# An LSH attention and two MoE layers on one core: both readers of a bucket-count bank on one engine, the scaled q written in one GpSimd pass, and a new written order

## The chip, the core and the metric

One core of one Trainium2 chip runs the whole program. The metric is device time in microseconds (us): the median of a few executions, each from launch to end. The engines are named as the profile names them: PE (TensorE, matmuls), PEld (its weight loads), DVE (VectorE), ACT (ScalarE), POOL (GpSimd) and SP (SyncE, which issues the DMAs). Each engine works through its own queue in order; they wait for one another through semaphores.

## The reference, cut to what matters

```python
# q, k, v: (2 batches, 8 heads, 768 positions, 64); proj: (64, 6)
q_bits = (q @ proj > 0);  k_bits = (k @ proj > 0)          # 6 bits = 64 buckets
mask   = q_bucket[:, :, :, None] == k_bucket[:, :, None, :]
scores = where(mask, q @ k.T / 8, -1e9)
attn   = exp(scores - max);  attn /= attn.sum() + 1e-9
x  = (attn @ v), heads joined: 1536 tokens x 512
x  = silu_moe(rmsnorm(x))      # 512 -> 1536 -> 512: gate, val, out
out = elu_moe(x)               # 512 -> 2048 -> 512: in, out
```

All of it is float32. The kernel gets that precision from fast matmuls by splitting an operand into a high part (rounded to the PE's fp32r type) and a low part (what the rounding lost).

## The kernel before, in words

The 16 heads are taken as 8 pairs (`j`); a pair has two heads (`a` = 0, 1). For each pair SP loads three layouts of q and k, and `prep` makes from them the operands of the score matmul. `prep_bits` (L434) projects q and k on PE (`ps_b`), and DVE turns the result into bits (`bitt`). `prep_count` (L455) multiplies the bits with a table on PE: each bank `ps_c` holds, for 384 positions, the number of agreeing bits with each of the 64 buckets, rows 0 to 63 for head 0 and rows 64 to 127 for head 1. Two instructions read such a bank, one for each head, and write the "hot" part of the operand: `tq` for i = 0 (q), `tk` for i = 1 (k). The engine of each of the two is `HOT[2 * i + a]` (L28, L479): before, head 0 of q and head 1 of k on DVE (L472), the others on ACT (L470). The program makes two readers of one bank on different engines wait for each other, in the written order.

`operand_k` (L369) writes the high part of k on ACT (L375) and the low part on POOL (L382). `operand_q` (L393) writes the high part of q. All 128 rows hold the same 64 dimensions twice; the upper 64 rows are to be q and the lower 64 rows q / 8. Before, POOL did this in two instructions, a plain cast of the upper half (L405) and a multiplication of the lower half (L412). SP then copies the lower half to its second place (`dup`, L416), and POOL replaces the upper half by the low part (L420).

`score` (L504) runs four matmuls `ps_s` for each 128 queries: the first two use the first plane of the operands (high and low parts), the other two the second plane (hot and `dup`). DVE takes the maximum (L524), ACT the exponential (L534). There are two double banks for `ps_s`, so the third score waits until the first exponential has read its bank. `turn` (L550) transposes the weights on PE (`ps_p`) and splits them on ACT (L570) and DVE (L574), for some units through POOL (L579 to L586). `weigh` (L597) multiplies with v (`ps_v`). After the attention come the norm and the two MoE layers (`ps_h`, `ps_y`, `ps_o`), which are nearly all matmuls.

What sets the order: every piece of work is a task, added to a plan with its engine and the keys that it reads and writes. `run` (L218) emits the tasks in the order of a written list of numbers, `ORDER` (L33); the costs in `plan.add` were used to find that list and do nothing at run time. The order on each engine's queue follows from it. A DMA that waits holds all later DMAs of SP's queue.

Of the kernel before, what the change touches and what calls it, by code (L numbers as in the profile page):

```python
# [27 lines left out]
HOT = ('DVE', 'ACT', 'ACT', 'DVE')  # L28
BW = (384, 512)
QENG = ["Pool"] * 16  # L30
# [195 lines left out]
def kernel(  # L226
# [76 lines left out]
    def dve(n):  # L303
        return n / 960.0 + 0.069
# [64 lines left out]
    def operand_k(j, a, cols, prio):  # L369
# [10 lines left out]
        def lo():  # L380
# [9 lines left out]
            [okey(j, a, 1, ("lo", h)) for h in cols], prio,  # L390
        )

    def operand_q(j, a, cols, prio, how):  # L393
        cs = slice(cols[0] * HS, (cols[-1] + 1) * HS)
        X_ = ("h3", "x", j, a, 2)
        n = HS * len(cols)
# [877 lines left out]
```

## Time and profile before

| | |
|---|---|
| median of 3 executions | 839.86 us (838.7 to 840.76) |
| profiled execution, its own time | 840.58 us |
| its span, first to last instruction | 838.8 us |
| PE busy | 816.9 us (97%) |
| DVE busy | 602.1 us (72%) |
| ACT busy | 416.8 us (50%) |
| POOL busy | 328.1 us (39%) |
| granted TensorE clock, mean over the span | 0.996 |

The shares are means over stages that differ. The first 280 us are the attention, in which PE, DVE, ACT and POOL are all busy most of the time; from there to the end PE is busy nearly without a break and the others have room. The end of a matmul is modelled, so that a short pause between two matmuls does not show as idle time. A granted clock of 1.00 stands for 2.4 GHz and 0.50 for 1.2 GHz.

### The profile page before, as it was taken

To read this page: it belongs to the slowest core of one execution; us is meant where nothing else is said; L and a number is where in the kernel's file an instruction comes from. 1 tells how busy PE (TensorE), PEld (TensorE's weight loads), DVE (VectorE), ACT (ScalarE), POOL (GpSimd) and SP (SyncE) were. 2 spreads that over 40 slices of the span, in tenths; PEclk is the share of its full clock that TensorE was granted. 3 is DMA by queue.
4 is the path that set the end of the run, shared out by engine and by line. 5 is a ranking of instruction groups with operands and counts; after the bars stand their busy time and mean duration, and the time that the engine had idled before them with its cause. 6 is when DMAs were issued, how large, how long until landed. Compare 5 with 4: busy or idle time off the path is not lost.

```text
span 838.8 us, 11843 instructions
## 1 busy us (share of the span) xinstructions
PE 816.9 (97%) x4498; PEld 714.1 (85%) x4498; DVE 602.1 (72%) x933; ACT 416.8 (50%) x785; POOL 328.1 (39%) x273
## 2 busy tenths in 40 slices
PE   7999999999899999999999999999999999999998
PEld 6898888888789999898888888888788888888887
DVE  4788899999998683543555564879666768677676
ACT  3898998977888553431222321335454242332321
POOL 7899987898988501100111212021012011110210
PEclk8999999999999999999999999999999999999999
DMA  6525842252103002200302123130322300021004
GB/s 214 165 68 169 275 143 83 67 159 69 39 1 114 1 1 93 71 26 1 131 21 76 51 61 115 39 103 13 111 76 87 102 24 26 26 76 50 1 1 150
DMA packets 28473, 64.99 MB, mean 77 GB/s; under 512 B 2816, under 2 KB 3584, under 8 KB 28416
## 3 DMA queue, kind: packets, MB, share of 16 engines
q1 hardware_dynamic: 28416, 64.24, 23.8%
q8 instruction: 35, 0.57, 0.3%
q14 instruction: 22, 0.18, 0.1%
HBM read 57.94 MB, written 3.15 MB: 73 GB/s over the span
## 4 chain that ended last, share of the span: by engine, by line
PE 77%; DVE 11%; ACT 7%; issue 2%; POOL 1%; DMA 1%; SPq 0%; ACTq 0%; DVEq 0%; POOLq 0%
PE ps_h L949 36%; PE ps_o L1089 15%; PE ps_y L1034 10%; PE ps_v L609 5%; PE ps_s L517 5%; PE ps_p L562 4%; DVE pt L574 2%; DVE nm L524 2%; ACT p L534 2%; ACT pt L570 2%; PE ps_b L442 1%; DVE wf L867 1%; DMA kk<-in_heads_dram 1%; DVE wf L874 1%; DVE ya L1046 1%
## 5 line engine op out<-in xcount | busy, mean ns | idle before, releaser
L900 POOL TENSOR_TENSOR wlo<-wf,whi 128x768 fp32r<-128x768 f32 (+1 forms) x54 | 88.4, 1650 | 448.3 <-ACT whi L896 387.4
L949 PE MATMUL ps_h<-xn,whi 128*128 128x512 f32 (+2 forms) x768 | 190.2, 336 | 0.0
L949 PEld LDWEIGHTS ps_h<-xn,whi 128*128 128x128 f32 x768 | 133.8, 189 | 11.9
L995 ACT CAST h<-hf 128x512 fp32r<-128x512 f32 (+1 forms) x87 | 52.1, 606 | 179.3 <-DVE hf L980 60.5
L949 PE MATMUL ps_h<-xn,wlo 128*128 128x512 f32 (+2 forms) x384 | 128.9, 336 | 0.0
L1089 PE MATMUL ps_o<-whi,h 128*128 128x512 f32 (+1 forms) x388 | 118.6, 387 | 0.4 <-DVE ya L1046 0.4
L949 PE MATMUL ps_h<-y,whi 128*128 128x512 f32 x384 | 118.2, 389 | 0.0
L517 PE MATMUL ps_s<-tk,tq 128*128 128x384 f32 x384 | 90.8, 359 | 8.7 <-ACT p L534 6.4
L609 PE MATMUL ps_v<-pt,vv 128*128 128x256 f32 x576 | 94.4, 294 | 2.1 <-DVE pt L574 1.0
L524 DVE TENSOR_REDUCE nm<-ps_s 128x1 f32<-128x768 f32 x96 | 90.8, 947 | 7.4 <-PE ps_s L517 6.5
L999 DVE TENSOR_TENSOR h<-hf,h 128x512 fp32r<-128x512 f32 (+1 forms) x87 | 64.5, 756 | 41.5 <-ACT h L995 41.3
L1034 PE MATMUL ps_y<-h,whi 128*128 128x512 f32 (+1 forms) x312 | 91.6, 374 | 0.8 <-DVE ya L1046 0.7
L534 ACT ACTIVATE p<-ps_s,nm 128x768 f32<-128x768 f32 x96 | 87.1, 908 | 8.5 <-DVE nm L524 7.7
L574 DVE TENSOR_TENSOR pt<-ps_p,pt 128x512 fp32r<-128x512 f32 x120 | 80.0, 682 | 12.9 <-ACT pt L570 12.0
L562 PE MATMUL ps_p<-ident,p 128*128 128x128 f32 x576 | 84.6, 278 | 2.9 <-DVE pt L574 2.2
L1089 PEld LDWEIGHTS ps_o<-whi,h 128*128 128x128 f32 x388 | 72.6, 188 | 15.5 <-DVE ya L1046 0.8
L974 ACT ACTIVATE sg<-ps_h 128x512 f32<-128x512 f32 (+1 forms) x87 | 49.4, 580 | 72.3 <-PE ps_h L949 53.3
L949 PEld LDWEIGHTS ps_h<-y,whi 128*128 128x128 f32 x384 | 72.1, 188 | 14.9
L609 PEld LDWEIGHTS ps_v<-pt,vv 128*128 128x128 f32 x576 | 78.8, 189 | 5.4 <-DVE pt L574 2.2
L562 PEld LDWEIGHTS ps_p<-ident,p 128*128 128x128 f32 x576 | 67.6, 142 | 12.0 <-DVE pt L574 5.1
L949 PEld LDWEIGHTS ps_h<-xn,wlo 128*128 128x128 f32 x384 | 72.6, 189 | 5.7
L517 PEld LDWEIGHTS ps_s<-tk,tq 128*128 128x128 f32 x384 | 64.3, 191 | 14.9 <-ACT p L534 10.8
(91 smaller groups left out, 1366.4 us busy)
## 6 DMA issues: line engine op xcount, KB each, us to landing
wraw<-in_moe_w_out_dram SPq DMA_DIRECT2D x12, 768.0 KB, 4.7
qq<-in_heads_dram SPq DMA_DIRECT2D x16, 384.0 KB, 4.2
qk<-in_heads_dram SPq DMA_DIRECT2D x16, 384.0 KB, 4.7
kk<-in_heads_dram SPq DMA_DIRECT2D x16, 384.0 KB, 4.0
wraw<-in_moe_w_in_dram SPq DMA_DIRECT2D x8, 768.0 KB, 5.6
wraw<-in_moe_w_out_dram SPq DMA_DIRECT2D x10, 512.0 KB, 3.6
vn<-in_v_dram SPq DMA_DIRECT2D x8, 384.0 KB, 3.5
wraw<-in_moe_w_gate_dram SPq DMA_DIRECT2D x4, 768.0 KB, 5.4
```

Of the source, the lines that this page charges most:

```text
L517: nc.tensor.matmul(st[B_][:, hf, 0:HS], lhsT=tq[:, x, c * 128:(c + 1) * 128], rhs=tk[:, x, hf * HS:(hf + 1) * HS], start=(x == 0), stop=(x ...
L524: nc.vector.tensor_reduce(out=st["nm", u, cc], in_=st[B_][:, :, 0:HS], axis=AX.XY, op=ALU.max, negate=True,)
L534: nc.scalar.activation(out=halves(st["p", u][:, cc]), in_=st.pop(B_)[:, :, 0:HS], func=AF.Exp, bias=st["nm", u, cc], scale=1.0, accum_out= ...
L562: nc.tensor.transpose(out=st[B_][:, o:o + 128], in_=p[:, cc, (2 * n + kt) * 128:(2 * n + kt + 1) * 128], identity=ident,)
L574: nc.vector.tensor_tensor(out=pt[:, 1], in0=st.pop(B_), in1=f(pt[:, 0]), op=ALU.subtract)
L609: nc.tensor.matmul(st[B_][:, 0:256], lhsT=st["vv", j][:, a, 2 * n + kt, :], rhs=pt[:, x, kt * 256:(kt + 1) * 256], start=(n == seq[0] and ...
L900: nc.gpsimd.tensor_tensor(out=l, in0=s["w"], in1=f(h), op=ALU.subtract)
L949: nc.tensor.matmul(ps[:, o:o + ln], lhsT=w[wp][:, kk, ft * 128:(ft + 1) * 128], rhs=t[xp][:, s:s + ln], start=(kk == 0 and n == 0), stop=( ...
L995: nc.scalar.copy(out=st["h", g, blk, ft][:, 0, 0:bw], in_=s["hf"])
L999: nc.vector.tensor_tensor(out=h[:, 1, 0:bw], in0=s["hf"], in1=f(h[:, 0, 0:bw]), op=ALU.subtract)
L1034: nc.tensor.matmul(s["ps"][:, 0:bw], lhsT=wo[wp][:, ft, m * 128:(m + 1) * 128], rhs=h[:, xp, 0:bw], start=(ft == 0 and i == 0), stop=(ft = ...
L1089: nc.tensor.matmul(s["ps"], lhsT=h[:, xp, t * 128:(t + 1) * 128], rhs=wo[wp][:, ft, ds], start=(ft == 0 and i == 0), stop=(ft == n - 1 and ...
```

## The change

Three things are edited. `HOT` gets one engine for each bank: DVE reads both heads of q, ACT both heads of k. `operand_q` writes the high part of q by one POOL instruction over 128 rows, with a factor for each row (`share`, 1 in the upper half and 1/8 in the lower) and a second factor of 1.0. `ORDER` is a new list; a few costs that were used to find it are changed too, and do nothing at run time. No matmul is added or taken away.

```diff
-HOT = ('DVE', 'ACT', 'ACT', 'DVE')
+HOT = ('DVE', 'ACT')
-QENG = ["Pool"] * 16
 ORDER = [
-    9, 0, 6, 5, 1, 7, 56, 50, 53, 2, 8, 48, 51, 57, 59, 49, 28, 10, 12, 13, 14, 15, 16, 17, 54, 55, 11, 60, 61, 68,
...
-    def operand_q(j, a, cols, prio, how):
+    def operand_q(j, a, cols, prio):
...
         def both():
-            nc.scalar.activation(
-                out=operand(j, a, 0)[:, 0, cs], in_=st["x", j, a, 2][:, cs], func=AF.Copy, scale=share[:, 1:2]
-            )
-
-        def upper():
-            out, in_ = operand(j, a, 0)[up, 0, cs], st["x", j, a, 2][up, cs]
-            nc.gpsimd.tensor_copy(out=out, in_=in_)
-
-        def lower():
-            out, in_ = operand(j, a, 0)[dn, 0, cs], st["x", j, a, 2][dn, cs]
-            if how == "mixed":
-                nc.scalar.activation(out=out, in_=in_, func=AF.Copy, scale=QSCALE)
-            else:
-                nc.gpsimd.tensor_scalar(out=out, in0=in_, scalar1=QSCALE, scalar2=None, op0=ALU.mult)
+            nc.gpsimd.tensor_scalar(
+                out=operand(j, a, 0)[:, 0, cs], in0=st["x", j, a, 2][:, cs], scalar1=share[:, 1:2], scalar2=1.0,
+                op0=ALU.mult, op1=ALU.mult,
+            )
...
-        if how == "ACT":
...
-            plan.add("Pool", 0.12 + n * 0.00092, upper, [X_], los, prio)
...
-                plan.add("Pool", 0.12 + n * 0.00092, lower, [X_], his, prio)
+        plan.add("Pool", 0.17 + n * 0.00105, both, [X_, "share"], his + los, prio)
...
         for a in range(2):
-            eng = HOT[2 * i + a]
+            eng = HOT[i]
```

Three places show what moves. The first is ACT at the start of the program, before the change; `tk` and `tq` are operands (110 and 101 of head 0, 131 and 134 of head 1), `kk` is loaded k, `ps_c` a count bank, `p` the weights.

```order
L375 ACTIVATE tk_110<-kk_108,share_86 128x384 [waits DMAHW4_49,DVE_49]
L375 ACTIVATE tk_110<-kk_108,share_86 128x384
L375 ACTIVATE tk_131<-kk_118,share_86 128x384 [waits DMAHW6_49]
L470 ACTIVATE tk_110<-ps_c_163 64x384 [waits PE_49]
L470 ACTIVATE tk_110<-ps_c_168 64x384 [waits PE_49]
L470 ACTIVATE tq_134<-ps_c_171 64x384 [waits PE_49]
L470 ACTIVATE tq_134<-ps_c_160 64x384
L534 ACTIVATE p_199,sums_200<-ps_s_183,nm_190 128x768 [waits DVE_49]
L534 ACTIVATE p_199,sums_200<-ps_s_192,nm_197 128x768 [waits DVE_49]
L375 ACTIVATE tk_131<-kk_118,share_86 128x384
```

ACT at the same place after the change (`tk_134` is of head 0, `tk_162` of head 1).

```order
L373 ACTIVATE tk_134<-kk_132,share_86 128x384 [waits DMAHW4_49,DVE_49]
L373 ACTIVATE tk_134<-kk_132,share_86 128x384
L451 ACTIVATE tk_134<-ps_c_142 64x384 [waits PE_49]
L451 ACTIVATE tk_134<-ps_c_152 64x384 [waits PE_49]
L451 ACTIVATE tk_162<-ps_c_152 64x384
L373 ACTIVATE tk_162<-kk_149,share_86 128x384 [waits DMAHW7_49]
L515 ACTIVATE p_184,sums_185<-ps_s_167,nm_172 128x768 [waits DVE_49]
L515 ACTIVATE p_184,sums_185<-ps_s_176,nm_182 128x768 [waits DVE_49]
L373 ACTIVATE tk_162<-kk_149,share_86 128x384
L451 ACTIVATE tk_162<-ps_c_142 64x384
```

The two `tq` readers are gone from ACT, and the cast of head 1's k (`kk_118`, now `kk_149`), which stood ahead of all readers of the counts, now stands behind three of them and ahead of the first exponential.

The second place is SP at the start, before the change: the loads, and the copies `tq<-tq` (`dup`).

```order
L322 DMA qq_89<-in_heads_dram 128x768
L322 DMA qk_92<-in_heads_dram 128x768
L1144 DMA pj_80<-in_proj_dram 128x256
L322 DMA qk_99<-in_heads_dram 128x768
L322 DMA kk_108<-in_heads_dram 128x768
L1137 DMA wtmp_116<-in_table_dram 128x256
L322 DMA kk_118<-in_heads_dram 128x768
L322 DMA qq_129<-in_heads_dram 128x768
L416 DMA tq_101<-tq_101 64x384 [waits DMAHW0_49,Pool_49]
L416 DMA tq_101<-tq_101 64x384 [waits DMAHW1_49,Pool_49]
L333 DMA vn_174<-in_v_dram 128x768 [waits DMAHW2_49]
L322 DMA qk_188<-in_heads_dram 128x768 [waits DMAHW3_49]
```

SP at the start after the change.

```order
L320 DMA qk_89<-in_heads_dram 128x768
L320 DMA qk_94<-in_heads_dram 128x768
L1125 DMA pj_80<-in_proj_dram 128x256
L320 DMA qq_127<-in_heads_dram 128x768
L320 DMA kk_132<-in_heads_dram 128x768
L1118 DMA wtmp_139<-in_table_dram 128x256
L404 DMA tq_129<-tq_129 64x384 [waits Pool_49]
L320 DMA kk_149<-in_heads_dram 128x768
L320 DMA qq_157<-in_heads_dram 128x768 [waits DMAHW0_49]
L331 DMA vn_165<-in_v_dram 128x768 [waits DMAHW1_49]
L404 DMA tq_129<-tq_129 64x384 [waits DMAHW2_49,Pool_49]
L320 DMA qk_236<-in_heads_dram 128x768 [waits DMAHW3_49]
```

Both `qk` now go first, `qq` of head 0 falls from the first place to the fourth, and the first `dup` stands ahead of the second `kk`, the second `qq` and `vn`, which wait in the queue until it has been issued.

The third place is PE at the counts of the last pair (some 214 us into the trace of before), before the change.

```order
L609 MATMUL ps_v_2823<-pt_2758,vv_1941 128x256 x4
L609 MATMUL ps_v_2823<-pt_2813,vv_1941 128x256 [waits Activation_49]
L609 MATMUL ps_v_2823<-pt_2813,vv_1941 128x256
L609 MATMUL ps_v_2823<-pt_2813,vv_1941 128x256 [waits DVE_49]
L609 MATMUL ps_v_2823<-pt_2813,vv_1941 128x256
L461 MATMUL ps_c_2842<-bitt1_83,wsel_81 128x384 [waits PE_49]
L461 MATMUL ps_c_2845<-bitt1_83,wsel_81 128x384 [waits DVE_49]
L461 MATMUL ps_c_2853<-bitt1_83,wsel_81 128x384 [waits Activation_49]
L517 MATMUL ps_s_2857<-tk_2465,tq_2342 128x384 [waits Activation_49]
L517 MATMUL ps_s_2857<-tk_2465,tq_2342 128x384 x3
```

PE at the counts of the last pair, after the change.

```order
L498 MATMUL ps_s_2796<-tk_2360,tq_2309 128x384 x4
L442 MATMUL ps_c_2803<-bitt1_83,wsel_81 128x384 [waits DVE_49]
L590 MATMUL ps_v_2808<-pt_2770,vv_1875 128x256 [waits DVE_49]
L590 MATMUL ps_v_2808<-pt_2770,vv_1875 128x256 x3
L590 MATMUL ps_v_2808<-pt_2745,vv_1875 128x256 x4
L442 MATMUL ps_c_2817<-bitt1_83,wsel_81 128x384 [waits DVE_49]
L442 MATMUL ps_c_2819<-bitt1_83,wsel_81 128x384 [waits PE_49,Activation_49]
L590 MATMUL ps_v_2808<-pt_2784,vv_1875 128x256 x4
L543 MATMUL ps_p_2827<-ident_79,p_2662 128x128 [waits DVE_49]
L543 MATMUL ps_p_2827<-ident_79,p_2662 128x128 x3
L442 MATMUL ps_c_2836<-bitt1_83,wsel_81 128x384 [waits DVE_49,PE_49]
L498 MATMUL ps_s_2849<-tk_2360,tq_2309 128x384 [waits Activation_49]
```

Three of the four `ps_c` stood in a row, with no other work between them and the next score; now at most two stand together, with `ps_v` and `ps_p` between, and a score ahead of all four.

## Rows read from the trace of the kernel before

**Rows 1.** Stretches: us, busy us (instructions) of each engine, PEclk, DMA share, GB/s.
```profile
14.90:21.70 6.80, 5.69 (x22) 5.09 (x21) 4.64 (x6) 3.45 (x7) 6.27 (x8) 0.50 0.27 76
20.00:120.00 100.00, 96.62 (x657) 87.33 (x656) 85.34 (x131) 87.96 (x179) 94.62 (x80) 0.99 0.54 171
120.00:260.00 140.00, 131.32 (x900) 117.25 (x900) 132.45 (x200) 118.12 (x242) 119.48 (x103) 1.00 0.21 63
280.00:820.00 540.00, 538.86 (x2667) 464.76 (x2667) 349.35 (x545) 185.10 (x319) 81.58 (x52) 1.00 0.17 54
```

**Rows 2.** Waits of PE: who waited for whom, us in total, times, longest.
```profile
PE ps_s L517 <- ACT p L534: 6.4, 9, 1.4
...
PE ps_s L517 <- DVE tq L472: 2.1, 1, 2.1
```

**Rows 3.** Waits of the bank readers for each other, in the same columns.
```profile
ACT tq L470 <- DVE tq L472: 5.9, 6, 1.3
...
DVE tq L472 <- ACT tq L470: 4.1, 4, 2.5
ACT tk L470 <- DVE tk L472: 3.7, 4, 1.5
...
DVE tk L472 <- ACT tk L470: 2.8, 3, 1.7
```

**Rows 4.** Timeline of the start: start us, us, engine, line, what, [idle before, releaser].
```profile
2.09 0.43 SPq L322 DMA_DIRECT2D qk<-in_heads_dram  x1
...
8.16 2.20 PE L442 MATMUL ps_b<-qk,pj 128*128 128x384 f32 x6 [0.77 <-DMA qk<-in_heads_dram]
...
9.18 1.12 ACT L375 ACTIVATE tk<-kk,share 128x384 fp32r<-128x384 f32 x2 [7.19 <-DMA kk<-in_heads_dram]
...
11.13 0.61 ACT L375 ACTIVATE tk<-kk,share 128x384 fp32r<-128x384 f32 x1 [0.83 <-DMA kk<-in_heads_dram]
...
12.52 0.87 ACT L470 ACTIVATE tq<-ps_c 64x384 fp32r<-64x384 f32 x2
...
13.42 0.55 DVE L472 TENSOR_SCALAR tq<-ps_c 64x384 fp32r<-64x384 f32 x1 [2.47 <-ACT tq L470]
...
14.07 1.55 PE L517 MATMUL ps_s<-tk,tq 128*128 128x384 f32 x6 [2.10 <-DVE tq L472]
...
16.73 2.93 PE L517 MATMUL ps_s<-tk,tq 128*128 128x384 f32 x8 [1.11 <-ACT p L534]
```

**Rows 5.** Groups by line and shape: count, busy us, mean ns, idle before.
```profile
L412 POOL TENSOR_SCALAR tq<-qq 64x768 fp32r<-64x768 f32 x14 | 29.9, 2133 | 1.2
...
L405 POOL CAST tq<-qq 64x768 fp32r<-64x768 f32 x14 | 11.9, 848 | 0.4
...
L412 POOL TENSOR_SCALAR tq<-qq 64x384 fp32r<-64x384 f32 x4 | 4.7, 1170 | 0.3
...
L382 POOL TENSOR_TENSOR tk<-kk,tk 64x384 fp32r<-64x384 f32 x4 | 3.9, 999 | 0.2
...
L741 POOL TENSOR_SCALAR z<-z 128x384 f32<-128x384 f32 x2 | 1.0, 514 | 0.2
```

**Rows 6.** The copies `tq<-tq` of L416, by line.
```profile
DMA to landing us min/median/max: 2.0/2.8/5.9
```

**Rows 7.** The loads of L322, by line.
```profile
DMA to landing us min/median/max: 2.8/4.4/8.6
```

**Rows 8.** Timeline at the counts of the last pair.
```profile
215.32 1.17 DVE L472 TENSOR_SCALAR tq<-ps_c 64x384 fp32r<-64x384 f32 x2
215.45 0.62 PE L461 MATMUL ps_c<-bitt,wsel 128*128 128x384 f32 x2 [1.04 <-DVE pt L574]
215.89 0.49 ACT L470 ACTIVATE tq<-ps_c 64x384 fp32r<-64x384 f32 x1 [1.14 <-DVE tq L472]
216.39 0.90 ACT L534 ACTIVATE p<-ps_s,nm 128x768 f32<-128x768 f32 x1
...
217.43 0.97 PE L517 MATMUL ps_s<-tk,tq 128*128 128x384 f32 x4 [1.36 <-ACT p L534]
```

More of the change, by code (lines that the diff above doesn't have):

```diff
@@ L422, in operand_q @@
         his, los, dups = ([okey(j, a, 0, (p, h)) for h in cols] for p in ("hi", "lo", "dup"))
-        if how == "ACT":
-            plan.add("ACT", act(n) + 0.15, both, [X_, "share"], his + los, prio)
-        else:
-            plan.add("Pool", 0.12 + n * 0.00092, upper, [X_], los, prio)
-            if how == "mixed":
-                plan.add("ACT", act(n) + 0.05, lower, [X_], his, prio)
-            else:
-                plan.add("Pool", 0.12 + n * 0.00092, lower, [X_], his, prio)
+        plan.add("Pool", 0.17 + n * 0.00105, both, [X_, "share"], his + los, prio)
         dma(dup, 64 * n * 4, his, dups, prio)
@@ L478, in prep_count @@
         for a in range(2):
-            eng = HOT[2 * i + a]
+            eng = HOT[i]
             plan.add(
-                eng, (act(HS) + 0.01 if eng == "ACT" else dve(HS)) + TURN * a, lambda a=a, eng=eng: hot(a, eng),
+                eng, (act(HS) + 0.01 if eng == "ACT" else dve(HS)) + (TURN + 0.1) * a, lambda a=a, eng=eng: hot(a, eng),
                 [B_], [okey(j, a, i, ("hot", hf))], prio + (0.01 if j else 1.0) * a,
@@ L496, in prep @@
                 operand_k(j, a, cols, prio + off("opk", j) + a * off("opa", j))
-                operand_q(j, a, cols, prio + off("opq", j) + a * off("opa", j), QENG[2 * j + a])
+                operand_q(j, a, cols, prio + off("opq", j) + a * off("opa", j))
     def unit(u):
@@ L541, in score @@
         need += [okey(j, a, 1, (p, hf)) for hf in range(2) for p in ("hi", "lo", "hot")]
-        plan.add("PE", 4 * mm(HS) + 0.02, pe, need, w, prio + off("S", j))
+        plan.add("PE", 4 * mm(HS) + 0.04, pe, need, w, prio + off("S", j))
         plan.add("DVE", dve(S), top, [B_], [N_], prio + off("max", j))
@@ L574, in lo @@
             nc.vector.tensor_tensor(out=pt[:, 1], in0=st.pop(B_), in1=f(pt[:, 0]), op=ALU.subtract)
-        plan.add("PE", 4 * 0.109, pe, [(P_, 0), (P_, 1), ("plim", u)], [B_], prio + off("T", j), duty=0.5)
+        plan.add("PE", 0.42, pe, [(P_, 0), (P_, 1), ("plim", u)], [B_], prio + off("T", j), duty=0.5)
         def keep():
@@ L630, in weigh @@
         plan.add(
-            "PE", 4 * mm(256) + 0.01, pe, [(T_, 0), (T_, 1), (V_, a, 0), (V_, a, 1)], [B_], prio + off("V", j)
+            "PE", 4 * mm(256) + 0.027, pe, [(T_, 0), (T_, 1), (V_, a, 0), (V_, a, 1)], [B_], prio + off("V", j)
         )
         if n == seq[-1]:
-            plan.add("ACT", act(256) + 0.13, evac, [B_], [(OT, a, i)], prio + off("my", j))
-            plan.add("DVE", dve(256) + 0.12, join, [B_], [(OT, a, i)], prio + off("my", j))
+            plan.add("ACT", act(256) + 0.25, evac, [B_], [(OT, a, i)], prio + off("my", j))
+            plan.add("DVE", dve(256) + 0.22 * a, join, [B_], [(OT, a, i)], prio + off("my", j))
     def post(j, prio, step):
@@ L652, in post @@
         sums = [(("sum", j), a, c) for a in range(2) for c in range(NC)]
-        plan.add("Pool", 0.12, plus, sums, [R_], prio)
+        plan.add("Pool", 0.32, plus, sums, [R_], prio)
         plan.add("DVE", 0.19, inv, [], [R_], prio)
@@ L1139 @@
     plan.add("ACT", 0.02, lambda: nc.scalar.preload_act_table_set("natural_log_exp_and_others"), [], ["tab"], -40, tab="exp")
-    plan.add("Pool", 1.22, setup, [], ["ident"], -30)
+    plan.add("Pool", 2.2, setup, [], ["ident"], -30)
     plan.add("DVE", 0.25, setup2, [], ["share"], -29.5)
@@ L1152 @@
     for n in range(WARM):
-        plan.add("PE", 0.218, lambda n=n: warm(n), ["ident"], [("bank", "warm")], 1e6)
+        plan.add("PE", 0.25, lambda n=n: warm(n), ["ident"], [("bank", "warm")], 1e6)
     dma(ld_table, 128 * 1024, [], [("h3", "wtmp")], -29.92)
```

278 rows, old and new, of the table ORDER are left out of this document.

## The prediction, written before the changed kernel ran

> **What bounds the kernel now.** I read the stretches first [rows 1]. From 280 to 820 us PE is busy 538.86 of 540 us, and the change leaves every matmul there as it is: nothing is to be won or lost in that part. From 20 to 120 us PE is busy 96.62 of 100, from 120 to 260 us 131.32 of 140, so the attention has some 12 us of PE idle time (3.4 + 8.7). In the later of the two stretches DVE is nearly as full as PE (132.45 of 140), in the earlier one POOL is (94.62 of 100). So a change to DVE, ACT and POOL work can act only through the pauses of PE before 280 us.
>
> The waits of PE say who ends them [rows 2]: the score waits for the exponential that frees its bank (6.4 us in 9 waits), and once, for 2.1 us, for the hot part of q on DVE. No row of that view after the start names POOL. The readers of the count banks wait for each other [rows 3]: 5.9 + 4.1 + 3.7 + 2.8 = 16.5 us of ACT and DVE time. The question is how much of this reaches PE. I followed it at two places where PE waits longest.
>
> **The start.** The first score is done late [rows 4]. The cast of head 1's k waits on ACT for its load until 11.13; behind it stand the readers of the counts, the two of q from 12.52; the DVE reader of q waits 2.47 us for ACT and runs at 13.42; the second half of the first score starts at 14.07, after PE has idled 2.10 us. The third score follows at 16.73, after the first exponential.
>
> After the change ACT reads only k's counts, ahead of head 1's cast, and DVE reads q's counts without waiting for ACT. What is late next? I go through everything the first score needs.
> - Loads seem to land by their place in SP's queue: the fourth issue of before (2.09) landed at about 8.16, the fifth at 9.18 [rows 4]. The `qq` of head 0 is now the fourth: 8.2 us.
> - The POOL pass over its first half then takes between 0.51 us (the one POOL multiplication with two factors in the trace, L741, on as many columns) and 1.17 us (L412, one factor, 64 rows) [rows 5]. I take 0.51, since two factors is the form that it has; done at 8.7.
> - The `dup` is issued then. Such copies land after 2.0 to 5.9 us, median 2.8 [rows 6]: 11.5, with 10.7 and 15.3 as ends. I take the median; at that time only the first `kk` and the table are still under way, where before four loads stood ahead of it.
> - ACT casts head 0's k from 9.18 to 10.30 as before; POOL's two low parts of k (1.00 each [rows 5]) follow at 9.75 and 10.75, done at 11.75.
> - DVE's hot q (0.55 [rows 4]) can start when the counts are there, about 11.0, done at 11.6; ACT's two of k are done by about the same time.
>
> So the first score could go on at 11.8 instead of 14.07: -2.3 us. But the cast of head 1's k now stands ahead of the first exponential on ACT, and its load waits in SP's queue behind the `dup`: issued at 9.2, landed after 2.8 to 8.6 us, median 4.4 [rows 7], that is at 13.6, and the cast takes 0.61. The exponential then starts at 14.2 at the earliest; the maximum that it needs is ready at about 13.6. The third score follows one exponential (0.90) later, at 15.1 instead of 16.73. I book **-1.6 us**. The ends: -2.3 if the load is quick; +2.6 if it takes 8.6 (17.8 + 0.6 + 0.9 = 19.3 against 16.73). A `dup` of 5.9 us behind a slow pass (15.3 for the first score) lies between the two.
>
> **The counts of the last pair.** Near 215 us PE waits 1.04 and then 1.36 us [rows 8]. The second wait is again the chain through the readers: ACT's reader of q waits 1.14 for DVE and takes 0.49, only then comes the exponential at 216.39, and the score at 217.43. Without that reader ahead of it the exponential could be 1.63 us earlier; a score was waiting for it 1.36. The order after the change also puts `ps_v` and `ps_p` between the counts. What is late next is DVE, which has both readers of q (1.17 us for two [rows 8]) and the maximum after them. I book **-1.4 us** of the 2.4; ends -2.4 and, if a bank now waits for a second reader on the same engine, +0.5.
>
> **The other bank readers.** Of the 16.5 us, 2.47 and 1.14 are used above; 12.9 us are left, spread over some 16 waits. They are DVE and ACT time, and PE had other work during most of them: in [rows 2] only the 2.1 us at the start names a reader. I book **-0.6 us**, with ends -2.0 and +4.4. The upper end is the price of the new arrangement: DVE now takes both readers of a q bank in a row, so a maximum behind the pair comes 0.55 us later; eight such pairs (four pairs of heads, two halves) lie in the last 140 us, where DVE has 7.55 us idle to cover them.
>
> **The POOL pass.** For the 14 wide ones, before: 2.133 + 0.848 = 2.98 us. After: 1.03 if two factors scale with columns from L741 (twice 0.514), up to 2.13 if the factor for each row costs what one factor costs [rows 5]. So POOL gets back 14 x 1.95 = 27 us, or 14 x 0.85 = 12 us; I take 27, from the row that has two factors. It is booked at **0** on the path, from -1 to +1: PE never waits for POOL, and POOL runs ahead of the scores by a pair. Its work is off the path at the start too, up to 0.66 us that the range above has.
>
> The rows say that one factor costs 2.5 times a cast of the same size. GPSIMD Engine Reference, in the Trainium skill (section "Performance versus the Vector engine"), says that a loop body of one or two operations is bound by the port, at 1.03 cycles an element, and only three or more cost more. By that rule a second factor changes nothing, and the pass would cost what L412 costs; the sum would be 0.6 us worse at the start, about 836.9. The rows speak against it, since L741 with two factors is faster than L412 with one, but no row has a factor for each row of the tile.
>
> **The new order elsewhere.** The DVE, ACT and PE queues keep the same pattern and the same share of weight preparation ahead of the last score; what swaps are neighbours. I book 0, from -3 to +4: PE's 12 us of pauses can shrink by a quarter, or grow as they did by 2.4 at one bad place.
>
> **Sum.** -1.6 - 1.4 - 0.6 = -3.6 us. Against the profiled execution (840.58: span 838.8 and 1.8 around it) this is 837.0; that one lies 0.7 above the median of 839.86, so I predict 836.3.
>
> **Rivals.**
> - *The clock at the start.* From 14.9 to 21.7 us PE is granted 0.50 and is busy 5.69 us [rows 1]; before that it had idled 2.10 us. If the shorter pause keeps the clock at 1.00, up to half of 5.69 = 2.8 us goes as well: 833.5. For it: the pause before shrinks. Against: PE must still wait for the exponential in the same place, and ACT and DVE work at that time bounds the gain. TensorE: Matmul & The Clock Gate, in the Trainium skill (Part 1, "The HAM clock gate"), has activity release the throttle, and its table of terms prices a throttled stretch at its length times one half: 3.4 us for 6.8, which would give 832.9. Chance 0.17.
> - *Hidden anyway.* What PE wins at the start and at 215 us is given back, because DVE at 95% from 120 to 260 us sets the pace and its work is not less: 838 to 840, say 839.3. For it: DVE's row in [rows 1]. Against: DVE itself idled 6.9 us for bank readers [rows 3]. Chance 0.24.
> - *Pairs of readers on DVE hold the maxima (slower).* All 16 q banks put 0.55 us ahead of a maximum, and the exponential and the score behind it slip with it: 16 x 0.55 = 8.8 - 3.6 = +5.2, 845.1. It decides once 12 or more of the 16 slip. For it: DVE's fill after 120 us. Against: at 215.32 DVE already ran two readers in a row, and from 20 to 120 us it has 14.7 us of room. Chance 0.13, with other regressions that the order could bring.
> - *The pass doesn't do what it is for*: the row-wise factor takes 2.13 us or more. 836.9 to 838 (0.6 us at the start, up to 1 us where POOL is 94.62 of 100 full). It lies inside the forecast's range and has a third of its chance, since the one row with two factors has none for each row.
>
> **How the numbers follow.** The forecast has 0.46, with its own range 832 to 839. About 0.3% (2.5 us) is what a measurement can tell from no change: below 837.3 is faster, above 842.4 slower. The forecast (836.3) and the clock rival lie on the faster side, 0.63 together; the hidden case is 0.24; slower is 0.13. The range 831 to 841.5 takes in the clock and the hidden case and leaves out most of the slower one.
>
> **What would show it.** Right: the second half of the first score starts near 11.8 us and the third score near 15.1; the rows of [rows 3] are gone or below 3 us in all; the POOL pass takes about 1.0 us on 768 columns; PE's wait at the last pair's counts is near 1 us; PE's idle time from 20 to 260 us falls from 12 to about 10. Wrong: the first exponential waits for head 1's k beyond 15 us; the pass takes 2 us or more; a new long wait of PE for DVE's maxima or for DVE's readers; or the clock at 0.50 in a second stretch.

## The result, and the profile after

The changed kernel takes 821.01 us (median of 4 runs, 820.28 to 821.39), the kernel before, run beside it, 840.11 us: a ratio of 0.977 [0.976, 0.979], 19 us less. Predicted were 836.3 us with a range of 831 to 841.5. The direction was right, the size and the range were not. A few executions of the kernels below took 60 us or more longer than the others of their kernel: medians and ratios leave them out, and of `e1`, `e4`, `e8` and `e16`, whose profiled execution was such a one (granted clock 0.75 to 0.85), the times alone are used.

The stretches of the changed kernel, in the columns of [rows 1]:

```profile
14.90:21.70 6.80, 5.95 (x37) 4.79 (x37) 4.45 (x6) 4.91 (x11) 6.58 (x10) 1.00 0.98 329
20.00:120.00 100.00, 99.77 (x715) 93.48 (x715) 93.60 (x144) 94.80 (x192) 80.39 (x76) 1.00 0.52 168
120.00:260.00 140.00, 135.35 (x955) 125.12 (x954) 132.12 (x205) 123.14 (x249) 118.93 (x106) 1.00 0.25 73
```

From 20 to 120 us PE had 3.4 us of idle time before and has 0.2 now: a gain of 3.2 by that column. But it issues 715 matmuls there instead of 657, 9% more, by their columns too, and the weight loads (PEld) went from 87.33 to 93.48. The column that looked full was not. POOL fell from 94.62 to 80.39, and the clock of the first row is 1.00 where it was 0.50. (From 246.8 us on, the third row holds the first layer, so it isn't like for like.)

The gain comes in evenly. I took the start of the same score in both traces: the 5th score is 3.5 us earlier, the 33rd 7.9, the 49th 9.1, the 73rd 12.5, the last one 17.8 (245.97 against 263.73 us). Another 3 us come in the layers (20.8 at their last `ps_h`), and the spans differ by 19.4. On the two pages PE's idle time falls from 21.9 to 11.9 us, and its busy time from 816.9 to 807.5 us for the same 4498 matmuls: about half of the gain comes out of the idle time and the other half out of the busy column.

The start, as timeline (columns as in [rows 4]):

```profile
7.65 0.59 POOL L397 TENSOR_SCALAR tq<-qq,share 128x384 fp32r<-128x384 f32 x1 [6.35 <-DMA qq<-in_heads_dram]
...
8.51 1.12 ACT L373 ACTIVATE tk<-kk,share 128x384 fp32r<-128x384 f32 x2 [6.51 <-DMA kk<-in_heads_dram]
...
10.18 1.14 DVE L453 TENSOR_SCALAR tq<-ps_c 64x384 fp32r<-64x384 f32 x2 [0.25 <-PE ps_c L442]
...
10.63 1.95 PE L498 MATMUL ps_s<-tk,tq 128*128 128x384 f32 x8
...
12.02 0.62 ACT L373 ACTIVATE tk<-kk,share 128x384 fp32r<-128x384 f32 x1 [0.56 <-DMA kk<-in_heads_dram]
...
12.89 0.90 ACT L515 ACTIVATE p<-ps_s,nm 128x768 f32<-128x768 f32 x1 [0.25 <-DVE nm L505]
...
13.94 0.96 PE L498 MATMUL ps_s<-tk,tq 128*128 128x384 f32 x4 [1.19 <-ACT p L515]
```

DVE idles only 0.25 us before it reads q's counts, for PE and not for ACT; the first two scores run in one piece from 10.63, and the third starts at 13.94 instead of 16.73. The cast of head 1's k, which I feared ahead of the exponential, starts at 12.02, 1.6 us sooner than I had put its load.

The waits of PE that name the attention's work (columns as in [rows 2]):

```profile
PE ps_s L498 <- ACT p L515: 1.7, 2, 1.2
PE ps_s L498 <- POOL vv L345: 1.7, 1, 1.7
...
PE ps_p L543 <- DVE pt L555: 0.8, 3, 0.4
...
PE ps_c L442 <- DVE tq L453: 0.7, 1, 0.7
```

The 6.4 us for the exponential [rows 2] are 1.7. One wait for POOL is new, 1.7 us near 181 us. No reader of a count bank waits for another reader any more, so the rows of [rows 3] have no counterpart. The wait of 0.7 us is at the counts of the last pair, where [rows 8] had 1.04 and 1.36; right behind it PE waits another 0.35 us for ACT's reader of k.

The pass of POOL, in the columns of [rows 5]:

```profile
L397 POOL TENSOR_SCALAR tq<-qq,share 128x768 fp32r<-128x768 f32 x14 | 12.8, 912 | 0.2
...
L397 POOL TENSOR_SCALAR tq<-qq,share 128x384 fp32r<-128x384 f32 x4 | 2.4, 589 | 6.6 <-DMA qq<-in_heads_dram 6.4
```

With 0.91 us it costs less than the multiplication alone (2.13 us) and nearly as little as the cast alone (0.85).

A view that I had not read before the prediction is the chain of waits, followed back from the last instruction of the program. For a stretch it gives the share that each line has on that chain. First the kernel before, from 20 to 120 us:

```profile
by line: PE ps_v L609 13.9%; PE ps_s L517 11.8%; PE ps_p L562 10.7%; ACT p L534 9.2%; ACT pt L570 8.4%; DVE pt L574 7.8%; issue 7.3%; DVE nm L524 7.0%; PE ps_b L442 3.9%; ACT wf L851 2.4%; DVE tq L472 2.4%; ACT tq L470 2.0%; ACT pf L579 2.0
```

The changed kernel in the same stretch:

```profile
by line: PE ps_p L543 23.6%; PE ps_s L498 23.0%; PE ps_v L590 22.8%; PE ps_b L423 7.7%; DVE nm L505 3.8%; DVE pt L555 2.3%; PE ps_c L442 2.3%; issue 2.2%; POOL sq L679 1.9%; POOL sq L675 1.5%; POOL pt L567 1.3%; DVE wf L835 1.1%; DVE tq L45
```

Before, the four PE lines hold 40% of the chain, though PE counts as 96.6% busy there; most of the rest goes round the loop of maximum, exponential, transposed weights and their splitting on DVE and ACT. After, five PE lines hold 79%, and neither exponential nor cast of ACT is among the lines shown. Over the whole span the pages give PE 77% of the chain before and 89% after.

### The profile page after: what moved, and what is told of

The parts are those of the page before. It is cut to its first block, busy times and chain, and to the rows that moved or that the text cites. A ratio compares the mean times of both kernels' runs of the same rounds, so it can differ in the third digit from the quotient of the medians.

```text
span 819.4 us, 11842 instructions
## 1 busy us (share of the span) xinstructions
PE 807.5 (99%) x4498; PEld 712.1 (87%) x4498; DVE 596.4 (73%) x933; ACT 417.1 (51%) x785; POOL 296.8 (36%) x255
## 4 chain that ended last, share of the span: by engine, by line
PE 89%; DVE 5%; DMA 2%; POOL 2%; issue 2%; ACT 1%; SPq 0%; DVEq 0%; POOLq 0%; ACTq 0%
PE ps_h L930 40%; PE ps_o L1070 16%; PE ps_y L1015 12%; PE ps_v L590 6%; PE ps_p L543 6%; PE ps_s L498 6%; DVE nm L505 2%; PE ps_b L423 2%; DVE pt L555 1%; DMA qk<-in_heads_dram 1%; DMA qq<-in_heads_dram 1%; PE ps_x L648 1%; DMA tq<-tq 0%; DVE tq L453 0%; PE ps_c L442 0%
## 5 line engine op out<-in xcount | busy, mean ns | idle before, releaser
L881 POOL TENSOR_TENSOR wlo<-wf,whi 128x768 fp32r<-128x768 f32 (+1 forms) x54 | 90.4, 1687 | 456.6 <-ACT whi L877 441.3
L980 DVE TENSOR_TENSOR h<-hf,h 128x512 fp32r<-128x512 f32 (+1 forms) x87 | 68.4, 803 | 41.7 <-ACT h L976 41.4
L590 PE MATMUL ps_v<-pt,vv 128*128 128x256 f32 x576 | 96.1, 294 | 0.4 <-ACT tk L451 0.4
L498 PE MATMUL ps_s<-tk,tq 128*128 128x384 f32 x384 | 88.2, 351 | 3.4 <-ACT p L515 1.7
L551 ACT CAST pt<-ps_p 128x512 fp32r<-128x512 f32 x120 | 68.6, 588 | 13.4 <-PE ps_p L543 11.2
L1070 PE MATMUL ps_o<-wlo,h 128*128 128x512 f32 (+1 forms) x194 | 75.0, 387 | 0.0
```

The costliest lines, as they stand in the source:

```text
L498: nc.tensor.matmul(st[B_][:, hf, 0:HS], lhsT=tq[:, x, c * 128:(c + 1) * 128], rhs=tk[:, x, hf * HS:(hf + 1) * HS], start=(x == 0), stop=(x ...
L551: nc.scalar.copy(out=st[T_][:, 0], in_=st[B_])
L590: nc.tensor.matmul(st[B_][:, 0:256], lhsT=st["vv", j][:, a, 2 * n + kt, :], rhs=pt[:, x, kt * 256:(kt + 1) * 256], start=(n == seq[0] and ...
L881: nc.gpsimd.tensor_tensor(out=l, in0=s["w"], in1=f(h), op=ALU.subtract)
L980: nc.vector.tensor_tensor(out=h[:, 1, 0:bw], in0=s["hf"], in1=f(h[:, 0, 0:bw]), op=ALU.subtract)
L1070: nc.tensor.matmul(s["ps"], lhsT=h[:, xp, t * 128:(t + 1) * 128], rhs=wo[wp][:, ft, ds], start=(ft == 0 and i == 0), stop=(ft == n - 1 and ...
```

## The experiments

Each run has its own runs of the kernel before beside it (839.3 to 839.9 us).

### Which of the three edits it is

`e1_readers_old_order`, `e2_pass_old_order` and `e3_both_old_order` put the edits one by one, and both, into the kernel before with its old order. `e4_order_alone`, `e6_order_and_readers` and `e5_order_and_pass` take the changed kernel and undo both edits, the pass, and the readers. In all kernels with the old order and the new pass, the tile of row factors (`share`) is written ahead of everything else. The cuts of code here and below are shortened.

```diff
-HOT = ('DVE', 'ACT', 'ACT', 'DVE')                      # e1, e3 (undone in e4, e5)
+HOT = ('DVE', 'DVE', 'ACT', 'ACT')
-    tensor_copy(upper);  tensor_scalar(lower, QSCALE)    # e2, e3 (undone in e4, e6)
+    tensor_scalar(all rows, share, 1.0)                  # at the place of the first of the two
```

> The kernel before, in its own written order, with one edit: both readers of a count bank on one engine (DVE for q, ACT for k). Theory A (the gain of 19 us is the new order's; an edit alone in an order that was not found for it brings little): 838 to 842 us. Theory B (the waits of the bank readers for each other, 16.5 us of ACT and DVE time, were what slowed PE): 826 to 832. Theory C (POOL's slow multiplication was what slowed the attention): 838 to 841.

> The kernel before, in its own written order, with one edit: the high part of q by one POOL pass with two factors, standing where the first of the two old instructions stood. Theory A (order): 836 to 841 us. Theory B (bank readers): 837 to 841. Theory C (POOL gets back some 31 us of the first 280, the dup copies and so the loads behind them in SP's queue go earlier): 824 to 832.

> The kernel before, in its own written order, with both edits. Theory A (order): 834 to 840 us, most of the 19 us missing. Theories B and C: 821 to 828, since either edit alone would carry most of the gain.

> The changed kernel in its new order, with both edits undone: the readers of a bank on DVE and ACT as before, and the high part of q by the two old POOL instructions (lower half first), one behind the other where the one pass stood. Theory A (order): 821 to 828 us. Theories B and C (the edits): 834 to 842, as the kernel before.

> The changed kernel, new order, with the readers of a count bank on two engines again (as before the change); the POOL pass stays. Theory D (the new order needs the fast POOL pass, since in it POOL is given less time ahead of each score): 821 to 826 us, nearly all of the gain kept. Theory E (it needs the readers on one engine): 836 to 842. Theory F (the new order was found for both, and each is worth about half): 828 to 834.

> The changed kernel, new order, with the high part of q by the two old POOL instructions (lower half first); the readers of a bank stay on one engine. Theory D (it needs the pass): 836 to 842 us. Theory E (it needs the readers): 821 to 826. Theory F (each half): 828 to 834.

| median us (ratio to before) | old order | new order |
|---|---|---|
| neither edit | 839.86 (before) | `e4` 842.34 (1.0027 [1.0014, 1.0041]) |
| readers alone | `e1` 842.12 (1.0018 [1.0005, 1.0032]) | `e6` 839.54 (1.0004 [0.9989, 1.0018]) |
| pass alone | `e2` 843.11 (1.0040 [1.0025, 1.0055]) | `e5` 832.96 (0.9921 [0.9893, 0.9948]) |
| both | `e3` 842.75 (1.0033 [1.0019, 1.0048]) | 821.01 (0.9774 [0.9757, 0.9791]) |

None of the three gains anything alone; each costs 2 to 3 us against the kernel before beside it (839.88), 0.4 to 4.6 by the intervals. Alone they sum to +2.2 + 3.2 + 2.5 = +7.9, together they give -19. What each is worth shows where the other two are there: 12 us for the readers (`e5` against the changed kernel), 18.5 for the pass (`e6`), and 21.7 for the order itself (`e3`). The two edits need each other as well: under the new order the readers give 2.8 us without the pass (`e4` to `e6`), and the pass 9.4 without the readers (`e4` to `e5`).

In `e2` POOL from 20 to 120 us falls from 94.62 to 74.89 and nothing is won:

```profile
20.00:120.00 100.00, 96.57 (x660) 86.96 (x658) 86.85 (x133) 88.98 (x180) 74.89 (x70) 1.00 0.54 172
```

So before the change POOL, full as it was, did not set the pace. In `e3` the readers no longer wait for each other, but for PE. DVE's groups up to 246 us, in the columns of [rows 5]:

```profile
L525 DVE TENSOR_REDUCE nm<-ps_s 128x1 f32<-128x768 f32 x87 | 82.2, 947 | 8.5 <-PE ps_s L518 7.8
L575 DVE TENSOR_TENSOR pt<-ps_p,pt 128x512 fp32r<-128x512 f32 x101 | 67.3, 681 | 11.1 <-ACT pt L571 10.3
L473 DVE TENSOR_SCALAR tq<-ps_c 64x384 fp32r<-64x384 f32 x32 | 17.4, 550 | 5.0 <-PE ps_c L462 4.4
```

The same groups of the changed kernel:

```profile
L505 DVE TENSOR_REDUCE nm<-ps_s 128x1 f32<-128x768 f32 x95 | 89.8, 947 | 3.5 <-PE ps_s L498 3.0
L555 DVE TENSOR_TENSOR pt<-ps_p,pt 128x512 fp32r<-128x512 f32 x112 | 74.6, 682 | 4.1 <-ACT pt L551 2.7
...
L453 DVE TENSOR_SCALAR tq<-ps_c 64x384 fp32r<-64x384 f32 x32 | 17.7, 553 | 1.3 <-PE ps_c L442 0.5
```

The means are equal to 3 ns; the idle time ahead of the three falls from 24.6 to 8.9 us, and DVE gets through 95 maxima instead of 87 in the same stretch. The new order moves no work off DVE: more often the input is ready when DVE comes to it.

`e3` also shows how far the chain can be trusted. Its stretch and its chain, from 20 to 120 us:

```profile
20.00:120.00 100.00, 95.66 (x655) 86.41 (x653) 85.70 (x130) 88.50 (x178) 74.79 (x70) 1.00 0.54 172
by line: PE ps_s L518 21.1%; PE ps_v L610 19.4%; PE ps_p L563 16.8%; PE ps_b L443 6.8%; ACT p L535 6.3%; issue 4.0%; ACT pt L571 3.8%; ACT tk L471 3.6%; DVE nm L525 2.6%; DVE pt L575 2.6%; PE ps_c L462 2.2%; ACT ot L624 1.7%; ACT wf L852 1.
```

Five PE lines hold 66% of it, where the kernel before had 40%, and nothing is won. So the chain says which lines the end hangs on, but PE's share of it is no measure of the time. The matmuls and the weight loads that get through the stretch go with the time better here: 655 and 86.41 us in `e3`, 657 and 87.33 before, 715 and 93.48 after the change.

With the readers split again (`e5`) the waits of [rows 3] are back, 11.0 us in all:

```profile
DVE tk L453 <- ACT tk L451: 4.4, 4, 1.9
...
DVE tq L453 <- ACT tq L451: 2.6, 2, 1.6
ACT tq L451 <- DVE tq L453: 2.5, 3, 1.3
ACT tk L451 <- DVE tk L453: 1.5, 1, 1.5
```

Under this order the split costs 12 us, about the length of these waits; how many of them lie on the chain was not followed. With POOL's two instructions back (`e6`) POOL is the chain, from 20 to 120 us:

```profile
by line: PE ps_v L589 11.7%; PE ps_s L497 10.6%; PE ps_p L542 8.6%; POOL tq L398 8.5%; POOL pt L566 7.7%; POOL tq L407 7.2%; DMA kk<-in_heads_dram 6.2%; issue 4.7%; POOL tk L380 4.6%; POOL tq L399 4.1%; POOL vv L345 3.9%; PE ps_b L422 3.9%;
```

and PE waits for it:

```profile
PE ps_v L589 <- POOL pt L566: 5.3, 6, 2.7
PE ps_s L497 <- POOL tk L380: 2.3, 3, 1.6
```

Six POOL lines hold 36% there; in the kernel before none was among the largest. The new order asks for operands sooner than the old POOL delivers them.

### Why the pass is fast

`e7_one_factor` keeps the pass with its factor for each row and leaves the second factor of 1.0 away.

```diff
-    scalar1=share[:, 1:2], scalar2=1.0, op0=ALU.mult, op1=ALU.mult,
+    scalar1=share[:, 1:2], scalar2=None, op0=ALU.mult,
```

> The changed kernel with the POOL pass over 128 rows and the factor for each row, but without the second factor of 1.0. If one factor is the slow form (2.13 us on 768 columns in the kernel before), the pass takes 2.1 us instead of 0.91 and POOL loses 14 x 1.2 + 4 x 0.6 = 19 us: by theory D 828 to 838 us, by theory E 821 to 823. If the factor for each row, not the number of factors, makes it fast, the pass takes 0.9 us and the time is 821.

827.55 us (0.9868 [0.9827, 0.9909]; three executions from 826.39 to 830.54), 6.5 us more than the changed kernel:

```profile
L397 POOL TENSOR_SCALAR tq<-qq,share 128x768 fp32r<-128x768 f32 x14 | 31.5, 2252 | 0.2
...
L397 POOL TENSOR_SCALAR tq<-qq,share 128x384 fp32r<-128x384 f32 x4 | 5.0, 1245 | 5.6 <-DMA qq<-in_heads_dram 5.4
```

2252 against 912 ns: it is the second factor that makes the pass fast. The factor for each row adds little: 2252 ns over 128 rows, against 2133 for one constant factor over 64 [rows 5].

### Where in the program the order gives its gain

Three kernels have both edits and the new order up to a point, and from there the old order of what is left: `e8_new_start` up to the 12th score, `e9_new_half` up to the 48th, `e10_new_attention` up to the 96th and last.

```diff
-ORDER = new
+ORDER = new[: up to the n-th score] + [t for t in old if t is not in that part]
```

> Both edits; the tasks up to the twelfth score (some 28 us) in the new order, all others in the old order. Between the first and the twelfth score the changed kernel won 4.0 us. Theory A (a better order wins what it wins in its own stretch, and keeps it): that off the old order with both edits (842.8), 838 to 840 us. Rival (an early gain is taken back by whatever sets the pace after it): 842 to 844.

> Both edits; the tasks up to the 48th of 96 scores (some 135 us) in the new order, all others in the old one. By its trace the changed kernel was 9.1 us ahead at that score. Theory A (each stage keeps what its own order wins): 842.8 - 9 - 1 = 832 to 835 us. Rival (the old order of the second half takes an early start back, as it did with 3 of the 4 us of the first twelve scores): 838 to 842.

> Both edits; the tasks up to the last score in the new order, what follows (the end of the attention, the norm, the two MoE layers) in the old one. In the traces the two layers alone took 3.3 us less after the change. If that is the new order of the layers: 823 to 826 us. If it only follows from how the attention ended: 820 to 822.

841.30 (1.0021 [1.0005, 1.0038]), 832.03 (0.9903 [0.9881, 0.9924]) and 824.24 us (0.9819 [0.9790, 0.9848]; one execution of four took 828.01). From `e3` (842.75) that is -1.5 for the start, which the intervals can't tell from nothing, -9.3 for the next 36 scores, -7.8 for the last 48, -3.2 for the tasks after the last score. Of the 4.4 us that the changed kernel is ahead at the 12th score most is given back when the old order follows at once. What the first half wins is kept: `e9` is ahead of the kernel before by 9.7 us at the 49th score and by 8.6 at the last.

### What DVE's time is worth

`e11_double_new` and `e12_double_old` (the latter from the kernel before) issue each DVE reader twice, 17.7 us more of DVE work.

```diff
-                nc.vector.tensor_scalar(out=to, in0=at, ...)
+                for _ in range(2):
+                    nc.vector.tensor_scalar(out=to, in0=at, ...)
```

> The changed kernel, with each DVE reader of a count bank issued twice (32 more instructions of 0.55 us, 17.7 us more DVE work, the same result written again). Theory G (in the new order DVE sets the pace of the attention, being 95% busy from 20 to 240 us): 12 to 18 us more, 833 to 839. Rival H (PE and the chain score, maximum, exponential set it, DVE has room): 2 to 8 us more, 823 to 829.

> The kernel before, with each DVE reader of a count bank issued twice (32 more instructions of 0.55 us). Theory G (here the written order sets the pace and DVE, 85 of 100 busy from 20 to 120 us, can take up some of it): 2 to 9 us more, 842 to 849. Rival H (DVE's price is the same under both orders): as much more as the changed kernel with the same edit.

838.99 (0.9995 [0.9980, 1.0009]) and 857.07 us (1.0211 [1.0176, 1.0247]): +18.0 and +17.6 us. At this place a microsecond of DVE costs about one microsecond, in either order. A part of it is the clock: it was granted 0.992 to 0.996 in `e11`, against 0.999 to 1.000 in the changed kernel. Executions of the kernel before average 838.7 us where the granted clock is 0.998, 839.7 at 0.996 and 842.2 at 0.992; by these, some 3 of the 18 us of `e11` are an estimate of that part. In `e12` DVE's two readers have 6.4 and 5.7% of the chain from 20 to 120 us, in the kernel before 2.4 and at most 2.0: the added work came to lie on the chain, whatever PE's busy column says.

Does work taken away pay as much? `e13_less_dve_new` (from the changed kernel) and `e14_less_dve_old` (from `e3`) move six maxima of the weight pieces, 0.63 us each, from DVE to POOL; `e15_no_max_new` and `e16_no_max_old` leave the same six out.

```diff
             def c2():
+                if g == 0:
+                    return          # e13, e14: issued on POOL right behind c1; e15, e16: not at all
                 nc.vector.tensor_scalar(out=s["w"], in0=s["w"], scalar1=LEAST, ...)
```

> The changed kernel, with the first DVE step of the six weight pieces that are prepared during the attention (a maximum over 768 columns, 0.65 us) done by POOL instead, directly behind ACT's step, as one pass with two factors. DVE has 3.9 us less to do before the last score, POOL some 5.5 us more. Theory K (DVE's time ends the attention in the new order: its work and its idle time add up to it, a microsecond for a microsecond): 3 to 4 us less, 817 to 818. Rival L (more DVE work costs its full time, but less DVE work only becomes DVE idle time, since PE and the order set the pace): 820 to 821.5.

> The kernel before in its old order with both edits (842.8 us), and with the same six DVE steps done by POOL. Theory K (what differs between the orders is DVE's idle time alone; DVE's work has the same price in both): 3 to 4 us less, 839 to 840. Rival L (in the old order DVE waits for others, so less work only becomes more waiting): 842 to 843.5.

> The changed kernel without six of its 54 maxima of weight pieces (the maximum with 2^-15 of the six pieces of the first group, which are prepared during the attention, is left out); nothing takes their place. DVE does 6 x 0.634 = 3.8 us less work before the last score. Theory K, DVE's own work is what ends the attention: 817 to 818 us, as doubling the readers cost 18 us for 17.7 us of work. Rival L, work taken from DVE under a written order only becomes idle time: 820 to 821.5 us.

> The same six maxima left out of the kernel with both edits in the old order (e3: 842.75 us); nothing takes their place. Theory K: 839 to 840 us. Rival L: 842 to 843.5 us. If the new order gives the time back and the old one does not, DVE's work is the limit under the new order only, which would be the difference between the two orders.

The first two came out at 832.78 (0.9921 [0.9908, 0.9934]) and 854.51 us (1.0178 [1.0165, 1.0192]), 12 us slower each, for a reason that I had not reckoned with. In `e13` the maximum takes 2.8 us on POOL:

```profile
L834 POOL TENSOR_SCALAR wf<-wf 128x768 f32<-128x768 f32 x6 | 16.7, 2776 | 9.0 <-ACT wf L832 8.0 <-DVE pt L555 0.9
```

and POOL stands still ahead of it until ACT has written the weights that it reads, while PE waits for POOL's later work:

```profile
PE ps_v L590 <- POOL pt L567: 6.0, 4, 5.0
...
POOL wf L834 <- ACT wf L832: 8.0, 3, 6.7
```

Here too a part is the clock (granted 0.992 to 0.994 in `e13`). The two decide nothing about DVE. `e15` gives 819.93 us (0.976 [0.974, 0.978]), `e16` 842.11 (1.0029 [1.0016, 1.0041]): 1.1 and 0.6 us less than the kernels they are made from, which the intervals can't tell from nothing, for 3.8 us of work. Up to 246 us DVE is busy 226.3 us in `e15` and 228.6 in the changed kernel: 2.3 us became idle time there. Two of its groups in `e15`:

```profile
L505 DVE TENSOR_REDUCE nm<-ps_s 128x1 f32<-128x768 f32 x95 | 89.8, 947 | 3.8 <-PE ps_s L498 3.2
L555 DVE TENSOR_TENSOR pt<-ps_p,pt 128x512 fp32r<-128x512 f32 x112 | 74.7, 683 | 5.3 <-ACT pt L551 3.9
```

The splitting now waits 5.3 us where it waited 4.1. So the theory that DVE's total work ends the attention falls: under a fixed order, work taken from a place that has little of the chain (1.1% for `DVE wf L835` in the changed kernel) mostly turns into waiting. Work added between a count and its score comes to lie on the chain: in `e11` the readers have 11.5% of it from 20 to 120 us, against at most 1.1% in the changed kernel.

No kernel here beats the changed one; `e15` leaves out part of the work.

## Why the prediction was wrong

**The budget: too small.** "The attention has some 12 us of PE idle time", and the change "can act only through the pauses of PE". PE's busy time held work that was spaced out: 58 more matmuls fit into a stretch that had 3.4 us free. The same row that I quoted [rows 1] has the weight loads, at 87.33 of 100, which left nearly four times as much (12.7 us); and Perfetto Trace Analysis, in the Trainium skill (section "Identifying the Most-Contended Engine"), says that the busy share of matmuls is not a good measure of the distance to the limit and that the busy share of weight loads is one to use. The rows agree: the loads rose by 7% where the matmul column rose by 3%, and the matmuls by 9%. The text ahead of the prediction said that short pauses don't show; I used the column as a budget all the same. But the budget alone did not make the sum small: of its 12 us I booked 3.6. The sign "PE's idle time from 20 to 260 us falls from 12 to about 10" failed: from 20 us to the last score it fell to 4.9.

**The new order elsewhere: booked 0, from -3 to +4; this is the step that failed.** I took its swaps for exchanges of neighbours and priced each edit against the old order. Alone the new order is +2.5 (`e4`), inside my ends. On top of the two edits it is -21.7 (`e3`). No sum of single prices can give -19 from +2.2, +3.2 and +2.5.

**The other bank readers: booked -0.6, from -2.0 to +4.4.** In the old order +2.2 for all readers (`e1`), inside my ends; in `e3`, which has the pass too, DVE's readers of q wait 4.4 us for PE's count, where they waited 4.1 us for ACT before, so a new wait took the place of the old one. In the new order with the pass -12 (`e5`).

**The POOL pass.** The duration was right: 1.03 us forecast, 0.91 measured. GPSIMD Engine Reference, in the Trainium skill (section "Performance versus the Vector engine"), has bodies of one and of two operations cost the same; `e7` has 2252 ns for one factor and 912 for two, so the measurement decides against it here. The duration was in part luck: line 741, which I read as two factors, multiplies by one constant and adds another. Its worth was wrong: booked 0 (from -1 to +1) because PE never waited for POOL. Under the old order nothing was won (`e2`, +3.2); under the new one, with the readers, 18.5 us (`e6`).

**The start: booked -1.6; the third score came 2.8 us sooner.** The mechanism was right (first readers without waits, no pause before the second half of the first score), the two loads and the `dup` were quicker than I took from medians. But as a term it was worth little: followed by the old order it leaves 1.5 us (`e8`), not clear of noise.

**The counts of the last pair: booked -1.4.** The pauses there fell from 2.4 to 1.1 us, -1.3. What that alone is worth was not measured.

**The rivals.** The clock: it happened, 1.00 in the stretch that had 0.50; it can't be more than a part of the 3.5 us by the fifth score. By the executions of the kernel before (839.7 us at a mean of 0.996, 838.7 at 0.998), going on to 1.00 is worth an estimated 2 of the 19 us. Hidden anyway: it came out so for each edit alone and for the start, not for the whole; its reason, that DVE's work sets the pace, does not fit `e15`. Pairs of readers holding the maxima: the price was right where time is added at the readers (`e11`: 1 us per us), but the maxima didn't slip: the idle time ahead of DVE's three groups fell instead.

What stays open is which of the swaps in the list carry the gain: `e8` to `e10` show only that it accrues along the attention, with 3 us behind it. That it works through inputs that are ready sooner is read from DVE's idle time, not from an experiment on one swap.

## What to carry to other kernels

Where a loop runs over several engines, don't take PE's idle time as the bound of what can be won: a PE that counted as 97% busy was given 9% more work, and the weight loads of the same stretch (87 of 100) left more room. The chain of waits names the lines that the end hangs on, but a larger share for PE alone is not yet time won (66% in `e3`). Price an edit that comes with a new order under that order: the pass cost 3.2 us alone under the old one and gave 18.5 under the new with the readers changed. Taking away the waits of two readers for each other gained nothing under the old order; putting them back under the new one cost about their length.

## What the runs showed of the hardware that I had not expected

On POOL a multiplication of 128x768 elements with one factor took 2.25 us and with two factors 0.91 us; a maximum by one constant with a multiplication by 1.0 behind it, on the same shape, took 2.78 us (2.87 in `e14`). A multiplication by one constant with an addition of another took 0.51 us on 128x384 (L741 [rows 5]), where the pass took 0.59. So it is not the number of operations alone that makes the form fast; only these pairs were measured.
